# Gated attention and routed experts on one core: three small moves in the order (block 38's scatters, stage 0's block sums, the turning of z)

## The chip, the cores and the metric

One Trainium2 chip, of which the kernel uses one core. The metric is the time of one execution on the device in microseconds (us), and less is better. Every time below is of that core. TensorE (PE) multiplies, VectorE (DVE) and ScalarE (ACT) work elementwise and read TensorE's sums out of PSUM, GpSimd (POOL) and SyncE (SP) mostly start transfers here, and ScalarE starts some as well.

## The reference

Two parts follow each other, all of it in fp32.

```python
# attention: u, v are 8 x 2496 x 256, z is 8 x 2496 x 64
scores = (1 / 2496) * z @ z.T            # per batch
out = maximum(scores, 0) ** 2 @ v
x = (u * out).reshape(19968, 256)
# experts: E = 8, D = 256, F = 1024
expert = token_ids * 2654435761 % 8
for e in range(8):
    mask = expert == e
    y[mask] = maximum(x[mask] @ w1[e], 0) @ w2[e]
```

## The kernel before

The whole program is one order written out by hand: each engine carries out its instructions in the order in which the source issues them, and waits only on data and on buffers that are still in use. A DMA waits also for an earlier one: the transfers that SP and ScalarE start take eight completion semaphores in turn, and each waits until the transfer that held its semaphore before has landed.

**Attention** takes 200 steps: 8 batches, in each of them 5 groups of queries g, in each of them 5 groups of keys s, so 25 steps a batch. A step is worth about 7.2 us. All products are made in the way of Strassen and Winograd: a 2 x 2 block product from 7 products, with block sums before and after. For a step:

- `score` (L251 to L264) makes z z^T on TensorE, relu and square on ScalarE and VectorE. Scores are symmetric, so only the groups with s >= g are made. Where s > g, VectorE transposes them too (`mirror`, L291, 8 transposes), SP stores the result in DRAM (`keep`, L299 and L303), and the later step that has s and g exchanged fetches it on ScalarE's queue (`recall`, L307).
- `sums` (L275 to L278) makes the four block sums t of the scores on VectorE. Scores, sums and mirrors stand two steps ahead of their use (`AHEAD = 2`).
- `attend` (L326) adds the 7 products with v to PSUM. After 5 steps `join` (L339 to L345) puts the products together.
- After that, the rows are turned (`gate`), go through DRAM, are multiplied by u (L389), and GpSimd scatters each row to a slot of its expert (`sort`, L411).

z must stand with its 64 features on the partitions, and twice, on partitions 0 to 63 and 64 to 127. For each batch it comes in four chunks of blocks of 32 rows, all of them during the batch before: `load_z` (L166, two DMAs on SP) loads a chunk, `turn_z` (L186 and L188) transposes it on VectorE, `copy_z` (L193, one DMA on SP) copies it to the other 64 partitions. Chunk c is loaded at step 5 + 4c of the batch before; the turn and the copy follow by a number of steps that the tuple below sets:

```python
for after, do in ((0, load_z), (5, turn_z), (6, copy_z)):
    c, due = divmod((g - 1) * NT + pos - after, 4)
```

**Experts.** The tokens lie in 40 blocks of 512 slots, each of one expert, and one small block of 128. Stage i does the up product of block i (`up_big`, L982: 14 products of two matmuls on TensorE, in two halves of 7) between the down products of block i-1 (7 products). The strings in `ORDER` fix how they alternate; each letter is one product:

```python
ORDER = {"first": "UUUUGUUUGUUUUUUU", "second": "DUDUDUUDUUDUU" "XUxUDUXUDUUUU", ...
         "end": "DDDDDDDd"}
```

"first" is stage 0, in which no down product is there yet; its G finishes the last rows of attention (L398 and L404), whose accumulators were still to be joined. Every set of 7 products ends up in `products`: the first product is copied by ScalarE (L944), and VectorE adds the others (L946 with product 6, L951 with 7, L952 with 5, L959 with 3, L962 with 4). They are made in the order 1, 6, 7, 5, 2, 3, 4. Product 2 is added onto product 1 in its PSUM bank and product 3 onto product 5, so product 3, the sixth, waits until VectorE has read product 5 (L952). After each half ScalarE has done relu, and VectorE makes the block sums of the hidden units (L993 to L996, tile `hs`), which the down products of the next stage read.

A down product has two forms. `down_big` (L1021, 4 matmuls of 256 columns) makes the output transposed; VectorE turns it (L1033, 4 transposes a block), GpSimd writes it to DRAM (L1037, 4 DMAs) and reads it back as rows (L1039), and scatters four tiles of 128 rows to the output (`store`, L934). `down_last` (L1053, 8 matmuls of 128 columns) has the hidden units as weights, so rows come out directly, in tile `o_last`, which has one buffer. It scatters two tiles as soon as its sixth product is joined (L959), two after the seventh (L962). Block 39 alone uses it. The small block's output (tile `o`) comes last: ScalarE's copy (L1090) and one scatter.

Of the kernel before, what the change touches and what calls it, by code (L numbers as in the profile page):

```python
# [24 lines left out]
def kernel(  # L25
# [10 lines left out]
    nc = tc.nc  # L36

    B, S, D = u.shape
# [18 lines left out]
    NL = E * -(-N // (E * BLK))  # L57
# [84 lines left out]
    FQ = FP // 2  # L142
# [582 lines left out]
    def big(j):  # L725
        return j < NL
# [6 lines left out]
    def half(j):  # L733
        return len(slot_tiles(j)) * P // 2
# [66 lines left out]
    def recall_early(i):  # L801
        if i < len(steps) and steps[i][2] < steps[i][1]:
            scores[i] = recall(*steps[i])
# [33 lines left out]
    for i, (b, g, s) in enumerate(steps):  # L837
        pos = i % NT
        to_keep, mirrors = mirrors, []
        if i:  # L840
            a = prepare_scores(i + AHEAD)
            recall_early(i + AHEAD + 1)
        for m in to_keep:
            keep(*m)
        if b + 1 < B:
            for after, do in ((0, load_z), (5, turn_z), (6, copy_z)):
                c, due = divmod((g - 1) * NT + pos - after, 4)
                if not due and 0 <= c < NZ:
                    do(b + 1, c)
        if pos == 0:  # L850
            acc = [acc_ps.tile([P, 2, W], F32, name="acc", tag="acc") for _ in range(4)]
        attend(b, g, s, ready.pop(i), acc, pos == 0, pos == NT - 1)
        if not i:
            a = prepare_scores(i + AHEAD)
            recall_early(i + AHEAD + 1)
        if i == len(steps) - 4:

            x_sb = rowpool.tile([P, 2, 2, D], F32, name="x_row", bufs=3)
            for _ in gate_at_once(*done, x_sb, lambda: mm_ps.tile([P, 2, D], F32, name="g_ps", tag="mm")):
                pass  # L860
            to_sort += [(*done[:2], x_sb, k) for k in range(4)]
        if 0 <= i - (len(steps) - 3) < SURE:
            for _ in turn_x(i - (len(steps) - 3)):
                pass
        if pos == NT - 1:
            done = (b, g, join(g, acc, opool if i < len(steps) - 1 else late, i == len(steps) - NT - 1))
        prepare_mirror(i + AHEAD, a)
        for c in range(max(b, 1), min(b + 2, B)):
            if i - c * PER in LOAD_V:
                load_v(c, LOAD_V[i - c * PER], nc.scalar)  # L870
            if i - c * PER in ADD_V:
                add_v(c, ADD_V[i - c * PER])
        if 0 <= i < NT - 2:
            add_v(0, i + 2)
        if pos == 0 and done is not None and i < len(steps) - NT:
            gated = gate(*done)
        if pos == 1 and gated is not None:
            put(*gated)
            put_at = i
            waiting.append(gated[:2])  # L880
            gated = None

        if i == len(steps) - NT:
            assert not [x for x in waiting + [y[1][:2] for y in fetched] + [y[:2] for y in to_sort] if x < (B - 1, LATE)]
            closing["z and mirrors"].close()
            gpool = pool("gpool", 2, side="right", reuse_waits="tile")
            late = closing["late"].enter_context(tc.tile_pool(name="late", bufs=1, side="right", reuse_waits="tile"))
            for j in range(SURE):
                load_x(j)
        if i in ROUTE and not is_routed:  # L890
            is_routed = next(routed, True) is True
            if is_routed:
                assert i < PREPARE[0] - 1

                rowpool = attention.enter_context(tc.tile_pool(name="rowpool", bufs=2))
        elif is_routed:
            if fetched and i >= fetched[0][0] + (5 if i < len(steps) - NT else 2):
                rows = fetched.pop(0)[1]
                multiply(*rows)
                to_sort += [(*rows, k) for k in range(4)]  # L900
            for _ in range(min(2, len(to_sort))):
                sort(*to_sort.pop(0))
            if len(fetched) < 2 and waiting and (i % PER in FETCH or i >= len(steps) - 5 * NT) and (len(waiting) > 1 or i > put_at + 1):
                fetched.append((i, fetch(*waiting.pop(0))))
        for _ in range((1 + (i % NT == 2)) * is_routed):
            if entered < C:
                enter(entered)
                entered += 1
        for part, after in enumerate((0, 3, 4, 6)):
            if i - after in PREPARE:  # L910
                prepare(PREPARE.index(i - after), part)
        if i == len(steps) - 20:
            load_w(0, 0)
        if i == len(steps) - 2:
            load_w(1, 0)
        if i == len(steps) - NT - 1:
            load_u(b, g)
        if i == len(steps) - 4:
            load_u(b, g, late)
# [43 lines left out]
        done(c21, 1, 0)  # L963
        yield

    def up_big(j):
        x, t = xT[j]
        y11, y12, y21, y22 = (x[:, h, c] for c in range(DP) for h in range(2))
        t1, t2, t3, t4 = (t[:, i] for i in range(4))
        n = half(j)  # L970
        h = hpool.tile([P, 2, 2, FQ, 2 * P], F32, name="h")[:, :, :, :, 0:n]
        sums = hpool.tile([P, 3, FQ, 2 * P], F32, name="hs")[:, :, :, 0:n]
        hid[j] = h, sums
        take = {1: (0, y11), 2: (2, y21), 3: (6, y22), 4: (3, t4), 5: (4, t1), 6: (5, t2), 7: (1, t3)}
        for f in range(0, FQ, 2):
            def made(m, ps):
                first = ps is None
                if first:
                    ps = up_ps.tile([P, 2, 2 * P], F32, name="h_ps", tag="held" if m in (1, 5) else "other")[:, :, 0:n]
                k, y = take[m]  # L980
                for r in range(2):
                    nc.tensor.matmul(ps[:, r], w1[j][:, k, ts(f + r, P)], y, start=first and r == 0,  # L982
                                     stop=True, skip_group_check=True)
                return ps
            r = rpool.tile([P, 2, 2, 2 * P], F32, name="r")[:, :, :, 0:n]
            c = lambda i, k: h[:, i, k, f:f + 2]
            yield from products(
                made, r[:, 0], r[:, 1], c(0, 0), c(0, 1), c(1, 0), c(1, 1),
                lambda o, i, k, ps=None: nc.scalar.activation(o, o if ps is None else ps, AF.Relu))  # L989

            x11, x12, x21, x22 = c(0, 0), c(1, 0), c(0, 1), c(1, 1)
            s1, s2, s4 = (sums[:, i, f:f + 2] for i in range(3))
            nc.vector.tensor_add(s1, x21, x22)  # L993
            nc.vector.tensor_sub(s2, s1, x11)
            nc.vector.tensor_sub(x21, x11, x21)
            nc.vector.tensor_sub(s4, x12, s2)  # L996

    def down_factors(j):
        h, sums = hid[j]
# [85 lines left out]
    def down_small(j):  # L1085
        ps = down_ps.tile([P, D], F32, name="o_ps", tag="any")
        for f in range(FP):
# [7 lines left out]

    ORDER = {"first": "UUUUGUUUGUUUUUUU", "second": "DUDUDUUDUUDUU" "XUxUDUXUDUUUU",
             "other": "UuUDUuUXDUdUDU" "UDUDUxUDUXUDU", "end": "DDDDDDDd"}

# [7 lines left out]
    for i in range(NL + 1):  # L1108
        parts = {}
        for j in at(i):  # L1110
            parts["U" if big(j) else "u"] = (up_big if big(j) else up_small)(j)
        for j in at(i - 1):
            parts["D" if big(j) else "d"] = (down_small if not big(j) else down_last if j == NL - 1 else down_big)(j)
        for j in at(i + 1):
            if i:
                parts["X" if big(j) else "x"] = turn_x(j)
        if i == 0:
            x_sb = late.tile([P, 2, 2, D], F32, name="x_row")
            parts["G"] = gate_at_once(*done, x_sb, lambda: down_ps.tile([P, 2, D], F32, name="g_ps", tag="held", bufs=2))
        for p in ORDER["first" if i == 0 else "second" if i == 1 else "end" if i == NL else "other"]:  # L1120
            next(parts.get(p, iter(())), None)
        for p in parts.values():
            assert next(p, None) is None and next(p, "end") == "end"
        if i == 0:
            for k in range(4):
                sort(*done[:2], x_sb, k)
            closing["late"].close()
            w2pool = pool("w2pool", 2, reuse_waits="tile")
            load_w(0, 1)
        for j in at(i + 2):  # L1130
            load_x(j)
        for m in range(2):
            for j in at(i + 2 - m):
                load_w(j, m)
# [5 lines left out]
    with tc.For_i(0, n_others, 1) as n:  # L1140
# [13 lines left out]
        h = hpool.tile([P, FP, P], F32, name="h1")  # L1154
# [42 lines left out]
```

## Time and profile before

| | before |
|---|---|
| median of 3 runs | 2437.59 us (2437.32 to 2439.12) |
| the profiled execution | 2437.5 us, its span 2435.7 us |
| granted clock of TensorE | 0.998 |
| busy: TensorE, VectorE, ScalarE, GpSimd | 2420.6, 1817.4, 728.5, 717.2 us |
| attention to experts | first expert product starts at 1444.79 us |
| last matmul ends | 2427.0 us |
| last scatter starts | 2430.69 us |

The profile is of one execution. In a line of the timeline the first number is the start and the second the duration (instructions of one kind that follow each other stand in one line), and in brackets stands the idle time of the engine before it and what ended that. A list of waits gives total, times and the longest.

### The profile page before, as it was taken

The numbers are of one execution on the slowest core, as the hardware profiler recorded it, in microseconds if no ns is written. First come the engines' busy times: TensorE is split into PE (matmuls) and PEld (weight loads), VectorE is DVE, ScalarE is ACT, GpSimd is POOL, SyncE is SP. The second block draws the span as 40 slices with busy tenths as digits, with TensorE's granted clock in tenths as the row PEclk, the third lists the DMA queues.
The fourth block names the chain that finished last, engine by engine and source line by source line (L and its number), as shares of the span: only waits on it lengthen the run. The fifth ranks groups of instructions, "written<-read, shape, count | busy, mean of one in ns | idle before, by whom it ended". The sixth has DMA issues, their size and how long they took to land. (4 is left out here: it accounts for less than half of the span.)

```text
span 2435.7 us, 32709 instructions
## 1 busy us (share of the span) xinstructions
PE 2420.6 (99%) x11191; PEld 2013.4 (83%) x11191; DVE 1817.4 (75%) x3811; ACT 728.5 (30%) x1210; POOL 717.2 (29%) x742
## 2 busy tenths in 40 slices
PE   9999999999999999999999999999999999999998
PEld 7787787787787787787787788888888888888887
DVE  7788778869869869768778667777777777777774
ACT  4324314324224224224224212222222222222221
POOL 0002013433534424513411121333232323232324
PEclk9999999999999999999999999999999999999999
DMA  7866667798888788778778677777767686867683
GB/s 151 204 204 188 162 193 234 238 282 243 256 265 253 252 251 255 243 221 245 253 216 258 188 230 232 223 256 221 260 213 264 217 260 215 261 219 256 224 269 116
DMA packets 425193, 559.59 MB, mean 230 GB/s; under 512 B 257372, under 2 KB 350381, under 8 KB 406592
## 3 DMA queue, kind: packets, MB, share of 16 engines
q1 hardware_dynamic: 350704, 326.23, 47.7%
q0 software_dynamic: 41872, 133.39, 15.7%
q10 hardware_dynamic: 32448, 97.86, 12.1%
q8 instruction: 88, 1.44, 0.2%
q14 instruction: 81, 0.66, 0.1%
HBM read 353.28 MB, written 200.26 MB: 227 GB/s over the span
## 5 line engine op out<-in xcount | busy, mean ns | idle before, releaser
L255 ACT ACTIVATE a<-s_ps 128x512 f32<-128x512 f32 (+1 forms) x480 | 246.9, 600 | 696.6 <-PE s_ps L251 614.6
L326 PE MATMUL acc<-t,vc 128*128 128x256 f32 (+3 forms) x1600 | 402.4, 374 | 0.3 <-DVE t L275 0.3
L411 POOL DMA_INDIRECT x_slots<-x_row,row x160 | 203.7, 1273 | 671.0 <-DVE x_row L389 558.7
L326 PEld LDWEIGHTS acc<-a,v_sb 128*128 128x128 f32 (+1 forms) x1600 | 293.2, 190 | 119.4 <-issue 52.7
L326 PE MATMUL acc<-a,v_sb 128*128 128x256 f32 (+3 forms) x1600 | 382.7, 382 | 0.3 <-DVE o L339 0.2
L326 PE MATMUL acc<-t,v_sb 128*128 128x256 f32 (+3 forms) x1600 | 369.7, 373 | 0.0
L326 PEld LDWEIGHTS acc<-t,vc 128*128 128x128 f32 (+1 forms) x1600 | 303.3, 190 | 34.4 <-DVE t L275 0.7
L326 PEld LDWEIGHTS acc<-t,v_sb 128*128 128x128 f32 (+1 forms) x1600 | 303.4, 190 | 33.6
L982 PE MATMUL h_ps<-xs,w 128*128 128x256 f32 x1280 | 316.1, 380 | 0.0
L1021 PE MATMUL o_ps<-h,w 128*128 128x256 f32 x1248 | 294.8, 379 | 0.0
L275 DVE TENSOR_TENSOR t<-a 128x512 f32<-128x512 f32 (+1 forms) x200 | 134.4, 672 | 202.4 <-ACT a L264 139.2
L989 ACT ACTIVATE h<-h 128x512 f32<-128x512 f32 x240 | 151.1, 630 | 420.6 <-DVE h L952 179.1
L982 PEld LDWEIGHTS h_ps<-xs,w 128*128 128x128 f32 x1280 | 243.6, 190 | 32.4
L1021 PEld LDWEIGHTS o_ps<-h,w 128*128 128x128 f32 x1248 | 243.2, 195 | 27.3
L251 PE MATMUL s_ps<-zT 64*128 64x512 f32 (+1 forms) x960 | 238.5, 614 | 0.5 <-DVE zT L186 0.5
L982 PE MATMUL h_ps<-xT,w 128*128 128x256 f32 x960 | 234.9, 380 | 3.3 <-DVE h L952 3.3
L1021 PE MATMUL o_ps<-hs,w 128*128 128x256 f32 x936 | 221.1, 379 | 0.0
L291 DVE STREAM_TRANSPOSE mirror<-a 128x256 f32<-128x256 f32 x640 | 217.8, 409 | 3.5 <-DMA scores<-mirror 2.3
L934 POOL DMA_INDIRECT out_dram<-o_sb,idx x156 | 159.2, 1021 | 186.4 <-DMA o_sb<-o 150.7
L662 POOL DMA_INDIRECT slot_tokens<-token,addr x160 | 170.9, 1068 | 133.5 <-DVE addr L650 85.1
L982 PEld LDWEIGHTS h_ps<-xT,w 128*128 128x128 f32 x960 | 182.5, 190 | 28.6 <-DVE h L952 4.1
L326 PE MATMUL acc<-a,vc 128*128 128x256 f32 (+3 forms) x800 | 201.1, 373 | 0.0
(184 smaller groups left out, 2620.1 us busy)
## 6 DMA issues: line engine op xcount, KB each, us to landing
w<-w_blocks SPq DMA_DIRECT2D x80, 1792.0 KB
scores<-mirror SPq DMA_DIRECT2D x192, 256.0 KB
a<-scores ACTq DMA_DIRECT2D x48, 1024.0 KB
scores<-mirror SPq DMA_DIRECT2D x224, 128.0 KB
a<-scores ACTq DMA_DIRECT2D x32, 896.0 KB
w_blocks<-w POOLq DMA_DIRECT2D x16, 1792.0 KB
xq<-x_slots SPq DMA_DIRECT2D x160, 128.0 KB
o<-y POOLq DMA_DIRECT2D x156, 128.0 KB
```

The source lines that it names most:

```text
L251: nc.tensor.matmul(flat(ps)[:, 0:2 * w].rearrange("p (q c) -> p q c", q=2), tile_of_keys(b, h, s, j), q_h, start=True, stop=True)
L255: nc.scalar.activation(of[:, :, j, h].rearrange("p m q e -> p q m e"), flat(ps)[:, 0:2 * w].rearrange("p (q m e) -> p q m e", q=2, e=in_bl ...
L275: nc.vector.tensor_sub(t1, y12, y11)
L291: nc.vector.transpose(to, in_blocks(a, g)[:, :, j, h].rearrange("p i q (r t) -> p t i q r", t=2)[:, t])
L326: nc.tensor.matmul(acc[k][:, half, 0:w], x[0:n, j, :], y[0:n, j], start=(first and j == 0 and half == 0), stop=(last and j == 1), skip_gro ...
L411: st = nc.gpsimd.indirect_dma_start(out=x_dram[:, :], out_offset=bass.IndirectOffsetOnAxis(ap=row[0:m, c:c + 1], axis=0), in_=x_sb[0:m, q, ...
L662: st = nc.gpsimd.indirect_dma_start(out=slot_dram[:, None], out_offset=bass.IndirectOffsetOnAxis(ap=addr[0:n, to:to + 1], axis=0), in_=tok ...
L934: st = nc.gpsimd.indirect_dma_start(out=out[:], out_offset=bass.IndirectOffsetOnAxis(ap=idx[:, col:col + 1], axis=0), in_=o, in_offset=Non ...
L982: nc.tensor.matmul(ps[:, r], w1[j][:, k, ts(f + r, P)], y, start=first and r == 0, stop=True, skip_group_check=True)
L989: lambda o, i, k, ps=None: nc.scalar.activation(o, o if ps is None else ps, AF.Relu))
L1021: nc.tensor.matmul(ps[:], w2_block(w2[j], k)[:, f], x[:, f], start=first and f == 0, stop=f == FQ - 1, skip_group_check=True)
```

## The change

There are three edits.

1. `down_last` serves the last two blocks, 38 and 39, instead of 39 alone. Block 38's 7 down products become 8 matmuls of 128 columns each, with the operands exchanged; its four transposes and its way through DRAM (5 DMAs on GpSimd) are gone; its four scatters start straight from `o_last`.
2. In stage 0 alone, the block sums of the hidden units are made once over all four columns (4 instructions of 128 x 1024) after the second half, instead of twice over two columns (2 x 4 instructions of 128 x 512), the first of which stood between the halves.
3. z's chunks are turned 3 steps after their load instead of 5, and copied 4 steps after it instead of 6.

Nothing else in the order is touched, apart from the completion semaphores, which are dealt out anew as transfers move or vanish.

```diff
-            for after, do in ((0, load_z), (5, turn_z), (6, copy_z)):
+            for after, do in ((0, load_z), (3, turn_z), (4, copy_z)):
...
-    def up_big(j):
+    def up_big(j, sums_last=False):
...
+        def add(a, b):
+
+            x11, x12, x21, x22 = (h[:, k, i, a:b] for i in range(2) for k in range(2))
+            s1, s2, s4 = (sums[:, i, a:b] for i in range(3))
+            nc.vector.tensor_add(s1, x21, x22)
+            nc.vector.tensor_sub(s2, s1, x11)
+            nc.vector.tensor_sub(x21, x11, x21)
+            nc.vector.tensor_sub(s4, x12, s2)
+
         for f in range(0, FQ, 2):
...
-            x11, x12, x21, x22 = c(0, 0), c(1, 0), c(0, 1), c(1, 1)
-            s1, s2, s4 = (sums[:, i, f:f + 2] for i in range(3))
-            nc.vector.tensor_add(s1, x21, x22)
-            nc.vector.tensor_sub(s2, s1, x11)
-            nc.vector.tensor_sub(x21, x11, x21)
-            nc.vector.tensor_sub(s4, x12, s2)
+            if not sums_last:
+                add(f, f + 2)
+        if sums_last:
+            add(0, FQ)
...
-            parts["U" if big(j) else "u"] = (up_big if big(j) else up_small)(j)
+            parts["U" if big(j) else "u"] = up_big(j, i == 0) if big(j) else up_small(j)
...
-            parts["D" if big(j) else "d"] = (down_small if not big(j) else down_last if j == NL - 1 else down_big)(j)
+            parts["D" if big(j) else "d"] = (down_small if not big(j) else down_last if j >= NL - 2 else down_big)(j)
```

## The prediction

> **What bounds the kernel now.** I read the page first, then TensorE's waits, then the timelines of three places: the seam between attention and experts, the tail, and the moments at which VectorE turns z.
>
> ```profile
> PE 2420.6 (99%) x11191; PEld 2013.4 (83%) x11191; DVE 1817.4 (75%) x3811; ACT 728.5 (30%) x1210; POOL 717.2 (29%) x742
> ```
>
> TensorE is busy for 2420.6 of 2435.7 us; 15.1 us are idle. The list of TensorE's waits says where (total, times, longest):
>
> ```profile
> PE h_ps L982 <- DVE h L952: 3.3, 2, 2.5
> ...
> PE o_ps L1053 <- DVE ro L946: 0.6, 1, 0.6
> ...
> PE acc L326 <- DVE t L275: 0.3, 1, 0.3
> PE acc L326 <- DVE o L339: 0.2, 1, 0.2
> ```
>
> The waits come to 6.3 us, and most of the rest, 8.7 us, is the tail after TensorE's last matmul (2435.7 - 2427.0). In attention it does not stand still: 0.5 us over 200 steps. So only the seam's 2.5 us and the tail can be won, and attention can only be lost. The profiled execution took 2437.5 us around its span of 2435.7, 0.1 from the median (2437.59); I sum against 2437.5. A measurement of this kernel can tell about 0.2% from no change, 4.9 us: faster means under 2432.7, slower over 2442.5.
>
> **Part one, stage 0's block sums.** TensorE's timeline at the seam (start, duration, last the idle time before):
>
> ```profile
> 1456.22 1.03 PE L982 MATMUL h_ps<-xT,w 128*128 128x256 f32 x4
> 1459.74 1.99 PE L982 MATMUL h_ps<-xT,w 128*128 128x256 f32 x4 [2.50 <-DVE h L952]
> 1461.52 1.90 PE L982 MATMUL h_ps<-xs,w 128*128 128x256 f32 x4
> 1463.23 1.92 PE L1021 MATMUL o_ps<-h,w 128*128 128x256 f32 x8
> ```
>
> VectorE meanwhile, and below it, from the table by stretch, the time after the gap (busy times of the engines; then granted clock, DMA share, GB/s):
>
> ```profile
> 1454.90 0.68 DVE L993 TENSOR_TENSOR hs<-h 128x512 f32<-128x512 f32 x1
> ...
> 1456.82 0.69 DVE L996 TENSOR_TENSOR hs<-h,hs 128x512 f32<-128x512 f32 x1
> 1457.42 0.68 DVE L946 TENSOR_TENSOR r<-r,h_ps 128x512 f32<-128x512 f32 x1
> ...
> 1459.00 0.69 DVE L952 TENSOR_TENSOR h<-h,h_ps 128x512 f32<-128x512 f32 x1
> 1459.80:1463.30 3.50, 3.50 (x9) 2.79 (x10) 0.69 (x1) 1.67 (x3) 0.00 (x0) 0.51 0.50 117
> ```
>
> Four sums (L993 to L996) stand for 2.52 us ahead of the three additions that release the bank TensorE needs. The edit moves them behind: L946 then begins at 1454.90, L952 ends at 1457.17, and the product that started at 1459.74 starts near 1457.22. It is due at 1457.09, so a wait of 0.14 stays, with the 0.10 that a start after a wait takes longer (1.13 instead of 1.03 after the 0.79 gap at 1450.94).
>
> The clock is the second term. After the gap the table shows 0.51 granted, over 3.5 us. Two products cost 1.78 and 1.71 us (from start to start, 1459.74 to 1461.52 to 1463.23) instead of 0.865: 1.76 more. After the 0.79 gap the next product followed 0.96 later, at full pace. The Trainium skill ("TensorE: Matmul & The Clock Gate", Part 1, HAM oscillation) warns of idle gaps over about 3.4 us only; by that rule the 2.50 gap would not be what halves the clock, the halving could stay, and the gain below would be 1.8 us smaller. The row halves it after 2.50, at once; I go by the row.
>
> What the edit adds comes later: four sums over 128x1024. The nearest row is L260's 128x1024 multiplication, 1.22 us each. With L962 over by about 1459.9, the first runs 1459.9 to 1461.1 and the second, which needs it, to 1462.3. It feeds block 0's second down product, now due at 1461.64 (1457.22 + 0.97 + 0.865 + 1.73 + 0.865): a new wait of 0.74 us plus 0.10, too short for the clock by the 0.79 row. It starts at 1462.4, where it started at 1465.85: **3.4 us gained**. The third sum (1463.5) comes before the third down product (1465.1). Bounds: 1.6 if the half clock stays, 4.0 if the sums overlap better. Weights in time: w2 of block 0 landed at about 1453.6.
>
> **Part two, block 38's way out.** The tail on GpSimd:
>
> ```profile
> 2410.45 2.68 POOL L1037 DMA_DIRECT2D o<-y  x4 [8.21 <-DVE y L1033]
> 2416.00 0.78 POOL L1039 DMA_DIRECT2D o_sb<-o  x1 [2.87 <-issue]
> 2420.38 1.04 POOL L934 DMA_INDIRECT out_dram<-o_sb,idx  x1 [3.60 <-DMA o_sb<-o]
> ...
> 2429.41 0.97 POOL L934 DMA_INDIRECT out_dram<-o_last,idx  x1 [0.30 <-issue]
> 2430.69 0.97 POOL L934 DMA_INDIRECT out_dram<-o,idx  x1 [0.30 <-issue]
> ```
>
> Nine scatters follow each other at 1.28 us from 2420.38: the queue is the limit, because block 38 goes through DRAM. Without the detour (5 transfers, 4 VectorE transposes) block 38's four scatters go at about 2406.6, 2407.9, 2410.0 and 2411.3, behind L959 and L962. Block 39's first two go at 2422.7 and 2423.9, after L959 (2422.25), the others at 2425.2 and 2426.5. GpSimd is free at 2427.5, and the last store waits for ScalarE's copy instead (2427.62 + 0.37): 2428.3 to 2428.4. The end follows the last store by 5.0 us (2435.7 - 2430.69). That is 2.3 to 2.4 us.
>
> Against it: block 38's 7 products become 8 matmuls of 128 columns. Down_last's products show 1.78 to 1.82 us, down_big's 1.73, so 0.05 to 0.09 each, 0.4 to 0.6 together. For it: VectorE's two transposes at 2409.38 (0.77 us) no longer delay L994, which keeps TensorE 0.3 us at 2412.1. TensorE ends 0.05 to 0.25 later. Net **2.25 us gained** (1.5 to 2.5). Both blocks share one o_last buffer: block 39's first write (L951, 2416.42) must wait for block 38's last scatter to have read, at 2411.3 + about 2.1, so 2413.5: 3 us of cover. Were it gone, L951 would hold TensorE's bank.
>
> **Part three, z turned and copied two steps sooner.** Nothing waits for z in time to be released, so the gain is none. The cost: the turn has 3 steps (7.2 us each) after its load instead of 5, and VectorE stands until the load lands. It already does at 5 steps (first VectorE's waits, then lines of the timelines of VectorE, ScalarE's queue and SP):
>
> ```profile
> DVE zT L186 <- DMA zn<-in_z_dram: 25.9, 7, 6.6
> 696.50 0.76 DVE L186 STREAM_TRANSPOSE zT<-zn 64x256 f32<-64x256 f32 x2 [7.54 <-issue]
> 683.62 0.38 ACTq L307 DMA_DIRECT2D a<-scores  x1
> 691.63 1.10 SPq L166 DMA_DIRECT2D zn<-in_z_dram  x2
> ```
>
> The third of four chunks (step 13 of a batch's 25) is the tight one; the others land 8 us or more ahead of their need. Behind the turn stand 8 mirror transposes and the next sum: 0.47 wake, 0.98 turn, 2.64 mirrors, 0.73 sum, together 4.82 us. TensorE needs that sum at 155.8, 335.1, 514.5, 693.8, 873.5, 1052.8, 1232.1 (batches 1 to 7), so z must be there 4.8 earlier. By the single packets it landed at 151.7, 330.4, 515.8, 696.0, 872.2, 1050.9, 1231.6. With these landings TensorE would stand 0.8, 0.1, 6.1, 7.0, 3.6, 2.9 and 4.3 us.
>
> But they will not be these. SP issues the load behind mirror stores, and a DMA waits for the transfer eight back that held its semaphore. In batches 3 to 5 that was the recall of step 21 (issued 683.62, z only at 691.63). With the copies moved, the order of semaphores shifts by one in the built program: the load now waits for the recall of step 20 at most, which landed at 146.2, 323.3, 503.6, 682.9, 862.4, 1042.0, 1221.6. Add 0.4 to issue, and 4.8 to 5.9 us of flight beside the next recall (batch 1: 146.94 to 151.72; batch 2: 324.50 to 330.40). Against the need that leaves 0 to 0.4 us of stall in each of the batches 1 to 5. Batches 6 and 7 flew 7.1 and 8.2 us behind three mirror stores that now go sooner; they come within need at up to 5.6 and 5.3 us. **0 to 1.5 us lost, taken as 0.3**, since most of the flights end within need. A load that met no recall flew 2.7 us (batch 5, 869.58 to 872.24), one beside it 5.9 (batch 2). The Trainium skill ("DMA: Bandwidth & Descriptors", Issuing engines are not separate DMA queues) says the same of all issuers: their transfers interleave on the same 16 engines; by it every load would fly 5.9 and the whole 1.5 us be lost.
>
> **The rivals.** *Slower: z lands too late.* If the loads land as before, the stalls add to 25 us, and five are over 2.5 us, so the clock adds five times 1.76: 33 us, about 2465; with some batches spared, 2445 to 2458. It decides once z lands over 6.0 us after the recall of step 20 in most batches. For it: VectorE waits 25.9 us today. Against it: that wait stems from a semaphore order that changes.
>
> *No change: the seam's wait only moves.* If the clock halves anyway, or the wide sums bring a wait that halves it again, part one gives 1.6: 2437.5 - 1.6 - 2.25 + 0.3 = 2434.0.
>
> *No change: the tail stays.* If o_last's reuse holds block 39, the last stores queue as before and part two gives nothing: 2434.4. The same band holds one or two late z loads (2436 to 2442).
>
> **How the numbers follow.** Forecast: 2437.5 - 3.4 - 2.25 + 0.3 = 2432.2 us, chance 0.55. Its own range is 2430.7 to 2435.9: all the better ends give 2437.5 - 4.0 - 2.5 = 2431.0, less 0.3 for the lowest run of before under its median; all the worse ones 2437.5 - 1.6 - 1.5 + 1.5. Of the 0.55, 0.47 lies under 2432.7. Seam or tail failing: 0.13; a few late z loads: 0.10; z late in most batches: 0.22. So faster 0.47, same 0.31, slower 0.22. The range goes from 2430.7 up to 2445, into the mildest of the slower cases, which leaves some 0.19 out.
>
> **What would show it.** Right: no wait over 1 us at the seam and no stretch at half clock there; GpSimd's last store on ScalarE's copy, without a queue before it; no `acc <- t` waits in attention. Wrong: TensorE waiting for t (L275) some 7 times, 150 to 1232 us in, each behind a late turn; or o_last's first addition ending an idle time of TensorE.

## The result: 1.4% slower, all of it in attention

| | before | after |
|---|---|---|
| median | 2437.45 us (2437.20 to 2439.12, 4 runs) | 2472.94 us (2472.07 to 2474.74, 4 runs) |
| the profiled execution, its span | 2437.5, 2435.7 us | 2472.07, 2470.2 us |

The ratio after to before is 1.0143, 95% interval 1.0129 to 1.0156. The forecast was 2432.2 us, its range 2430.7 to 2445, and the rival "z lands too late" was priced at about 2465. One execution of an experiment's kernel (e10) took 3776 us at a granted clock of 0.63; it is not in the ratio given for that kernel.

The page of the changed kernel: TensorE's busy time, which counts a product at half clock as a longer one, grew by 10.0 us, the span by 34.5.

```profile
PE 2430.6 (98%) x11247; PEld 2021.0 (82%) x11247; DVE 1815.3 (73%) x3803; ACT 727.7 (29%) x1210; POOL 696.1 (28%) x737
```

TensorE's list of waits (total, times, longest) has the line that the prediction named as its refutation. Before, the first two lines read 0.3 and 0.2, once each, and the third did not exist:

```profile
PE acc L326 <- DVE t L275: 16.0, 7, 3.4
PE acc L326 <- DVE o L339: 7.6, 6, 4.6
PE acc L326 <- DVE addr L650: 3.8, 1, 3.8
...
PE o_ps L1028 <- DVE hs L981: 0.6, 1, 0.6
```

VectorE's list names what it stood for; before it was 25.9 us in 7 waits (and 7.5 us in one put down to "issue"). Two of the waits, 4.7 us together, stand at the program's start in both kernels:

```profile
DVE zT L186 <- DMA zn<-in_z_dram: 107.7, 14, 13.3
```

One such place, batch 4, in the timelines of VectorE and TensorE, and in the table by stretch around it (granted clock third from the end):

```profile
711.49 0.77 DVE L186 STREAM_TRANSPOSE zT<-zn 64x256 f32<-64x256 f32 x2 [13.25 <-DMA zn<-in_z_dram]
712.19 0.36 DVE L188 STREAM_TRANSPOSE zT<-zn 64x224 f32<-64x224 f32 x1
712.48 2.68 DVE L291 STREAM_TRANSPOSE mirror<-a 128x256 f32<-128x256 f32 x8
715.09 0.64 DVE L275 TENSOR_TENSOR t<-a 128x512 f32<-128x512 f32 x1
...
715.79 2.08 PE L326 MATMUL acc<-t,vc 128*128 128x256 f32 x4 [3.39 <-DVE t L275]
717.66 1.53 PE L326 MATMUL acc<-a,vc 128*128 128x256 f32 x4
719.02 1.03 PE L326 MATMUL acc<-t,vc 128*128 128x256 f32 x4
...
715.20:718.60 3.40, 2.81 (x7) 2.28 (x8) 3.37 (x8) 0.00 (x0) 0.32 (x1) 0.51 0.87 191
```

VectorE stands 13.25 us for the chunk, then does the turn, the eight mirror transposes and the first sum, and TensorE waits for that sum. What follows the wait runs at half clock for 3.4 us.

The seam and the tail went as said. TensorE at the seam, then GpSimd's last scatters:

```profile
1493.56 2.12 PE L992 MATMUL h_ps<-xT,w 128*128 128x256 f32 x8
1495.52 1.03 PE L992 MATMUL h_ps<-xs,w 128*128 128x256 f32 x4
1496.38 1.89 PE L1028 MATMUL o_ps<-h,w 128*128 128x256 f32 x8
1498.11 1.03 PE L992 MATMUL h_ps<-xT,w 128*128 128x256 f32 x4
1499.72 1.99 PE L1028 MATMUL o_ps<-hs,w 128*128 128x256 f32 x8 [0.59 <-DVE hs L981]
```

```profile
2445.43 1.03 POOL L934 DMA_INDIRECT out_dram<-o_last,idx  x1 [0.30 <-issue]
2457.30 0.97 POOL L934 DMA_INDIRECT out_dram<-o_last,idx  x1 [10.84 <-issue]
...
2462.41 0.97 POOL L934 DMA_INDIRECT out_dram<-o,idx  x1 [0.30 <-ACTq L1148]
```

The 2.50 us gap is gone, 0.59 us came; and GpSimd's last four tiles start when block 39 is ready, no longer behind block 38's. The span split at landmarks of the timelines gives the account:

| stretch | before | after | difference |
|---|---|---|---|
| start to the end of attention's last product with v | 1444.95 | 1483.02 | +38.07 |
| to block 0's second down product | 20.90 | 16.70 | -4.20 |
| to the end of TensorE's last matmul | 961.18 | 961.59 | +0.41 |
| to the start of the last scatter | 3.66 | 1.10 | -2.56 |
| to the end of the span | 5.01 | 7.77 | +2.76 |
| sum | 2435.70 | 2470.18 | +34.48 |

Of the 38.07, TensorE's waits in attention make 27.0 (27.2 against 0.2, without the 0.3 for t at the program's start that both kernels have). The records of the granted clock hold six stretches of half clock in attention, 23.9 us together, each beginning in such a wait or up to 1.1 us after it; half of that time, less the idle part of it, is the other 11. The forecast took the last row as unchanged.

### The profile page after: what moved, and what is told of

It is laid out like the page before. It is cut to its first block, busy times and chain, and to the rows that moved or that the text cites. A ratio compares the mean times of both kernels' runs of the same rounds, so it can differ in the third digit from the quotient of the medians.

```text
span 2470.2 us, 32786 instructions
## 1 busy us (share of the span) xinstructions
PE 2430.6 (98%) x11247; PEld 2021.0 (82%) x11247; DVE 1815.3 (73%) x3803; ACT 727.7 (29%) x1210; POOL 696.1 (28%) x737
## 4 chain that ended last, share of the span: by engine, by line
PE 90%; DMA 4%; DVE 3%; issue 1%; SPq 1%; ACT 0%; POOL 0%; ACTq 0%; DVEq 0%; POOLq 0%
PE acc L326 42%; PE h_ps L992 19%; PE o_ps L1028 19%; PE s_ps L251 9%; DMA a<-scores 2%; DMA zn<-in_z_dram 1%; DVE mirror L291 1%; PE o_ps L1060 1%; DMA x_row<-x 0%; DVE t L275 0%; DVE t L277 0%; DVE t L276 0%; DMA x<-x_sb 0%; DMA zT<-zT 0%; DMA v_sb<-in_v_dram 0%
## 5 line engine op out<-in xcount | busy, mean ns | idle before, releaser
L326 PE MATMUL acc<-t,vc 128*128 128x256 f32 (+3 forms) x1600 | 408.7, 378 | 19.8 <-DVE t L275 16.0
L411 POOL DMA_INDIRECT x_slots<-x_row,row x160 | 185.3, 1158 | 707.5 <-DVE x_row L389 592.0
L1028 PE MATMUL o_ps<-h,w 128*128 128x256 f32 x1216 | 287.3, 379 | 0.0
L1028 PEld LDWEIGHTS o_ps<-h,w 128*128 128x128 f32 x1216 | 236.8, 195 | 26.5
L1028 PE MATMUL o_ps<-hs,w 128*128 128x256 f32 x912 | 215.5, 379 | 0.6 <-DVE hs L981 0.6
```

The lines of the kernel that those rows point to most:

```text
L326: nc.tensor.matmul(acc[k][:, half, 0:w], x[0:n, j, :], y[0:n, j], start=(first and j == 0 and half == 0), stop=(last and j == 1), skip_gro ...
L411: st = nc.gpsimd.indirect_dma_start(out=x_dram[:, :], out_offset=bass.IndirectOffsetOnAxis(ap=row[0:m, c:c + 1], axis=0), in_=x_sb[0:m, q, ...
L1028: nc.tensor.matmul(ps[:], w2_block(w2[j], k)[:, f], x[:, f], start=first and f == 0, stop=f == FQ - 1, skip_group_check=True)
```

## The experiments

Each was run beside the kernel before on the same chip; the medians of before in the five groups were 2438.6, 2438.5, 2439.8, 2441.0 and 2439.0 us, with single runs from 2435.9 to 2452, so a difference of 1 us is not told by a median here, and I go by the ratio's interval and by the profile.

**The three edits apart.** First z alone (e1), on the kernel before:

```diff
-            for after, do in ((0, load_z), (5, turn_z), (6, copy_z)):
+            for after, do in ((0, load_z), (3, turn_z), (4, copy_z)):
```

> The kernel before with z turned 3 and copied 4 steps after its load, nothing else. Theory A (all of the loss is z): the expert part starts 38.1 us later, as in the changed kernel, so 2437.5 + 38 = 2475 us (2472 to 2478), with six stalls of TensorE of 2.3 to 3.8 us for t and half clock behind each. Rival B (the loss needs the new tail or the new sums as well, through the completion semaphores dealt out anew): under 2460 us.

Measured 2472.6 us, ratio 1.0132 (1.0117 to 1.0148); attention ends at 1482.93 us, 38.0 later than before. Theory A holds: z is the whole loss. (How it is shared among the waits differs from one execution to the next: 0.5 to 4.8 us each.)

Then the expert edits with z as before (e2; in the changed kernel the tuple goes back to 5 and 6), the seam alone (e3; also `down_last if j >= NL - 1`), and the tail alone (e4; e2 with `up_big(j)`, so without sums last):

> The changed kernel with z turned and copied at 5 and 6 steps, as before. Theory A: attention as before, the seam 4.2 us shorter, block 38 0.4 longer, the last store 2.6 sooner behind TensorE: 2437.5 - 6.4 = 2431.1 us; if the end of the program again waits 2.9 us longer for a fetch of instructions (theory F), 2434.0. Rival B (part of the loss is in the expert part): over 2437.5.

> Only stage 0's block sums moved behind its products. Theory: the wait of 2.50 us and the two products at half clock are gone, a wait of 0.6 comes: 2437.5 - 4.2 = 2433.3 us, the end of the program as before. Rival (the forecast's sum was right and the surplus of 0.8 in the changed kernel was chance): 2434.1. Rival (the wide sums cost later stages): 2436 or more.

> Only block 38 through the row form. Theory: TensorE ends 0.4 us later, the last store starts 2.2 sooner. If the long drain at the end (3.7 instead of 0.9 us) belongs to GpSimd's shorter program, 2437.5 - 2.2 + 2.9 = 2438.2 us; if it came from other edits or by chance, 2435.3.

Measured: seam and tail together (e2) 2436.8 us, ratio 0.9988 (0.9979 to 0.9997); the seam alone 2436.8, 0.9989 (0.9980 to 0.9998); the tail alone 2438.0, 0.9994 (0.9985 to 1.0003). That is a gain of about 0.1% in the first two, so rival B falls; the intervals hold the expected gains of 3.5 us (e2 with the long end) and 4.2 us (e3), but the medians say 1.8 in both. In the third no difference can be told. The profiles add what the times hide. In all three, attention ended 1.8 to 3.4 us later than in the profile of before, although nothing in it was changed (the waits of TensorE there, for the join near 700 us and for z's copy near 733 and 914 us, 0.3 to 0.8 us each, make 0.9 to 1.4 us of it; the rest is not accounted for); before's own runs on that chip spread over 8 us. The last row of the account is 7.75 us in both kernels with the new tail and 5.03 in the one without. And the seam of the tail-only kernel, which has the old sums and the old gap, looks like this:

```profile
1460.50 1.13 PE L992 MATMUL h_ps<-xT,w 128*128 128x256 f32 x4 [2.50 <-DVE h L952]
1461.46 1.03 PE L992 MATMUL h_ps<-xs,w 128*128 128x256 f32 x4
1462.33 1.89 PE L1028 MATMUL o_ps<-h,w 128*128 128x256 f32 x8
```

The same 2.50 us gap, and full clock behind it: the stretch to the second down product takes 18.16 us, not 20.90. So of the gain of 4.20 only 1.5 is surely the edit's. The half clock made 1.8, in executions in which it comes; the other 0.9 is a wait of 0.79 us of the profile of before, at 1450.94, which e4 and the changed kernel lack and the seam-only kernel has (0.95).

**What makes z late.** Four kernels, all with the expert edits. Only the copy goes back (e5), `(3, turn_z), (6, copy_z)`:

> The changed kernel with z still turned at 3 steps, but copied at 6 as before. Theory A (VectorE's turn stands ahead of the block sums and waits for a load that has not landed): no better than the changed kernel, 2470 to 2476 us, six or seven waits of TensorE for t. Rival C (SP stands at the early copy and holds mirror stores and with them recalls): the loss is gone, about 2434 us.

Measured 2475.1 us, 1.0129 (1.0101 to 1.0156), VectorE's wait for z 107.2 us, TensorE's for t 17.3. Rival C falls: it is the turn in VectorE's queue, not the copy in SP's.

One step more lead (e6), `(4, turn_z), (5, copy_z)`:

> The changed kernel with z turned at 4 and copied at 5 steps, one step (about 7 us) more than in the change. Theory A: in the changed kernel TensorE stood 2.3 to 3.8 us a batch, and 7 us more cover that, so TensorE does not wait for t, and the time is that of the change without z: 2434 to 2437 us. Rival D (it is not the load's landing but the new order of semaphores, which is about the same here): 2455 us or more.

Measured 2441.2 us, 0.9998 (0.9984 to 1.0013): nearly all of the 35 us are back; the ratio lies 0.0010, some 2 us, above that of the expert edits alone. VectorE waits 57.7 us for z, and TensorE stands 2.0 to 2.7 us in three batches, so the expected absence of stalls was wrong by a little; rival D falls. One step is worth almost the whole loss, which is what a threshold looks like.

The load two steps sooner as well (e7), `(-2, load_z), (3, turn_z), (4, copy_z)`:

> The changed kernel with the loads two steps sooner as well, so that the turn is 5 steps behind the load as before, at the place of the change. Theory A: the third chunk is then loaded at step 11, ahead of the three recalls of steps 19 to 21; no stall, 2434 to 2437 us. Rival E (the place of the turn and the copy itself costs, whatever the lead): 2455 us or more.

Measured 2434.9 us, 0.9980 (0.9967 to 0.9993). VectorE's list:

```profile
DVE zT L186 <- DMA zn<-in_z_dram: 4.6, 2, 3.8
```

These two are at the program's start; in the steps VectorE does not wait for z at all. The place of the turn costs nothing, so rival E falls. The third chunk alone back at 5 and 6, the others at 3 and 4 (e8):

```diff
-            for after, do in ((0, load_z), (3, turn_z), (4, copy_z)):
+            for after, do in ((0, load_z), (3, turn_z), (4, copy_z), (5, turn_z), (6, copy_z)):
...
-                if not due and 0 <= c < NZ:
+                if not due and 0 <= c < NZ and (not after or (c == 2) == (after > 4)):
```

> The changed kernel with only the third chunk of z turned and copied at 5 and 6 steps again, the other three at 3 and 4. Theory A with the forecast's claim that the third chunk alone is tight: 2434 to 2437 us. Rival (the other chunks are late as well, as VectorE's waits of 6 us for the fourth chunk in batches 6 and 7 suggest): 2440 to 2455 us.

Measured 2439.0 us, 0.9992 (0.9979 to 1.0005). The claim holds for the loss: without the third chunk it is gone to within what can be told. It does not hold to the letter: VectorE waits 60.8 us in 16 pieces now, the fourth chunk among them (4 to 10 us each), and one wait of TensorE of 2.4 us for a sum is left.

The load sooner, the turn where it was before, `(-2, load_z), (5, turn_z), (6, copy_z)` (e10); and the early load and turn alone on the kernel before, without the expert edits (e12):

> All the edits to the experts, z loaded two steps sooner and turned and copied where it was before, so that the turn is 7 steps behind the load. Theory A: nothing waits for z; 2434.9 us as with the early turn (2433.5 to 2436.5). Rival (the early turn itself gains, for it takes VectorE's 34 us of waits out of the way): 1 us or more slower than that.

> The kernel before with z loaded, turned and copied two steps sooner, nothing else. Theory A: with its lead kept, the earlier turn costs nothing, and since VectorE no longer stands for z (33 us before), the small waits of TensorE in attention of some executions go too: 2438.5 - 0 to 2 us. Rival E (an early turn costs by its place): over 2445.

Measured 2437.0 us, 0.9984 (0.9971 to 0.9996), and 2437.5, 0.9990 (0.9980 to 1.0000). Between e10 and e7's 0.9980 no difference can be told, and e12 is not slower than before: the earlier turn, once its data is there, neither gains nor costs anything measurable. Only the lead counts.

Then the question why three steps, 21 us, are not enough for a load whose flight takes 3 to 11 us. The load stays at its step and moves to ScalarE's queue (e14, the changed kernel otherwise):

```diff
-                    do(b + 1, c)
+                    do(b + 1, c, *([(nc.scalar,)] if do is load_z else []))
```

> The changed kernel, z's loads of the later batches started on ScalarE's queue instead of SP's, at the same step of the order, turned and copied at 3 and 4. Theory H (3 steps are enough; the load is late because SP's queue stands some 30 us behind the order, at mirror stores that wait for the recall of step 20): the third chunk is issued some 30 us sooner against TensorE's step, VectorE does not wait for it, no wait of TensorE for t, 2434 to 2438 us. Rival (the flight itself beside recalls and stores is too long for 3 steps): the stalls stay, over 2455 us.

Measured 2433.0 us, 0.9969 (0.9956 to 0.9982), with the change's own turn at 3 steps: better than both kernels of the case. The third chunk of batch 2, SP's issue and VectorE's turn in the changed kernel, then ScalarE's issue in this one:

```profile
331.32 0.88 SPq L166 DMA_DIRECT2D zn<-in_z_dram  x2
339.15 0.77 DVE L186 STREAM_TRANSPOSE zT<-zn 64x256 f32<-64x256 f32 x2 [10.35 <-DMA zn<-in_z_dram]
```

```profile
288.11 0.96 ACTq L166 DMA_DIRECT2D zn<-in_z_dram  x2
```

Written at the same step, started 43 us sooner (35 us sooner against TensorE's step 13, since the changed kernel was 8 us behind by then); it landed at 293.1 and was turned at 320.6 without a wait. Over the seven batches ScalarE starts this chunk 36 to 46 us ahead of the times of SP in the profile of before. Theory H holds: the lead in steps was there, but SP's queue is late (it starts the load of step 13 32 to 40 us after TensorE began that step in the profile of before, 29 to 35 us in that of the changed kernel), as it stands at stores and loads whose semaphores the recalls hold. SP's list of waits in the changed kernel has these three among its lines:

```profile
SPq L303 <- DMA a<-scores: 205.0, 23, 13.1
SPq L299 <- DMA a<-scores: 146.4, 15, 14.4
SPq L166 <- DMA a<-scores: 40.8, 6, 14.9
```

The first two are the mirror stores, the third is z's load itself. The semaphores are dealt out anew in e14 as well, so it does not tell apart what the other queue brought and what the other semaphores brought. The flights are not short (5.0 to 11.0 us in this kernel), only no one waits for them.

**Where the tail's 2.56 us went.** GpSimd's sequencer ends the program with a drain. From its records, after the last scatter's start:

| kernel | drain begins | lasts | span ends |
|---|---|---|---|
| before, e1, e3, e11, e12 | 3.3 | 0.89 | 5.0 |
| after, e2, e4 to e10, e14 (all with the new tail) | 3.2 | 3.75 | 7.75 |

The early z and the seam without the new tail (e11: e7 with `down_last if j >= NL - 1`), for what the tail is worth:

> The kernel with early loads, without the new tail: z loaded, turned and copied two steps sooner, and the seam's sums last. If the new tail is worth nothing, since the drain takes 2.7 us of the 2.6 that the scatters gain and TensorE ends 0.3 later, it takes as long as with the tail: 2434.5 to 2435 us; if the tail is worth the forecast 2.25 us, 2437.

Measured 2434.8 us, 0.9978 (0.9968 to 0.9989), against 0.9980 with the tail: the new tail is worth nothing that can be told. Four kernels ask why. Two clearings ahead of the last scatter, `nc.gpsimd.memset(fill[:], 0.0)`, on e7 (e9):

> The kernel with early loads and all the edits (e7), with two clearings of a 128x1024 tile on GpSimd (0.94 us each in the profile of before) put ahead of the very last scatter. In every profile with the new tail the program ends 7.75 us after the last scatter's start, in every one without it 5.0. Theory G (the end hangs on GpSimd's sequencer, which runs ahead of a busy engine but stands at ScalarE's copy when the queue is empty): the last scatter starts 1.9 us later, the drain is again short, and the end comes 5.0 after the start: 2.7 - 1.9, that is 0 to 1 us sooner than without the clearings, at about 2434. Theory F (the shorter program ends in a fetch or the like): the drain stays at 3.7 us and the end comes 1.9 us later, 2436.8.

Measured 2436.3 us, 0.9990 (0.9981 to 0.9999); the drain stays at 3.75 us, the end at 7.75. The sequencer did not run ahead of the clearings (it read its next operand 0.5 us before the scatter's start, as with an empty queue), so this spoke for F without excluding G. The old tail with copies ahead of ScalarE's last one, eight (e13) and then sixteen (e15):

```diff
+        for _ in range(16):
+            nc.scalar.copy(fill[:].rearrange("p (f n) -> p f n", f=4), hid[j][:, 0:4])
         nc.scalar.copy(o[:], ps[:])
```

> The kernel before (old tail, GpSimd's program unchanged) with eight copies of 128x512 on ScalarE (0.6 us each by L989's row) ahead of the small block's last copy, so that GpSimd's scatter queue runs empty and its sequencer stands at ScalarE's copy. ScalarE's eight copies can begin only after the hidden units of the small block, so the last copy comes 0 to 5 us later. Theory G (the long drain comes when the last scatter is let go late by ScalarE, whatever the program): the end lies 7.75 us after the last scatter's start. Theory F (it belongs to the shorter GpSimd program of the new tail): 5.0 us after it.

> As the kernel with eight copies on ScalarE ahead of the last one (e13), with sixteen: there the last copy ended at 2431.4, still before GpSimd's turn for the last scatter at 2432.66. Eight more, 0.6 us each, put it near 2436, with GpSimd's queue empty since 2432.4. Theory G (a late release makes the long drain): the end 7.75 us after the last scatter's start, near 2444. Theory F (the program with the new tail has it, whatever the release): 5.0 to 5.2 us, near 2441.5.

With eight the last scatter still kept its turn (one execution, 2439.7 us), which decides nothing. With sixteen (one execution, 2438.5 us; the copies began early, so the last one ended at 2431.37, not at 2436) the scatter did wait for ScalarE with the queue empty:

```profile
2430.05 0.98 POOL L934 DMA_INDIRECT out_dram<-o_last,idx  x1 [0.30 <-issue]
2431.64 0.97 POOL L934 DMA_INDIRECT out_dram<-o,idx  x1 [0.62 <-ACTq L1143]
```

The drain took 0.89 us and the end came 5.02 us after the start. A late release does not make the long drain, so G falls. Last, e14 with five transfers put back on GpSimd (e16):

```diff
+        if j == NL - 2:
+            spare = nc.dram_tensor("spare", (5, P, P), F32)
+            for k in range(5):
+                nc.gpsimd.dma_start(out=spare[k], in_=ident[:])
```

> The kernel with z's loads on ScalarE's queue (e14), and in place of block 38's five transfers that the new tail removed, five of 64 KB from a constant tile to a spare tensor, on GpSimd behind block 38's scatters (they add nothing to the output). Theory F (the long drain comes with the shorter program): the drain is 0.9 us again and the time 2.9 us less, 2430.1. Theory G: the drain stays at 3.7 us and the time at 2433.

Measured 2432.5 us, 0.9971 (0.9959 to 0.9984): GpSimd has its 725 transfers of before again, and the drain takes 4.15 us. That it hangs on their number falls too, and with it theory F in the form of a shorter program. A fetch of instructions does not part the two cases by itself: the records of DMA packets hold one 2.3 to 2.4 us after the last scatter's start in all eleven profiles with the long drain, but also one at 2.05 us (e15) and one at 3.74 us (e1) with the short drain. The long drain is in every profile with the new tail (eleven of eleven) and in none of the seven without; what in it does that stays open.

## Why the prediction was wrong, point by point

- **What bounds the kernel: right.** Attention could only be lost, and it was.
- **Part one: right in kind, the clock term not as argued.** The wait for the second sum came as forecast (0.59 us, 0.74 expected); L946 to L952 run as placed, and even the 0.14 us wait ahead of product 3 came: products 2 and 3 at 1493.56 take 2.12 us together instead of 1.89, that is 0.13 of wait and 0.10 for the start after it (waits under 0.15 us are not listed). The gain was 4.20 us for 3.4, but 0.9 of it is luck, a wait that the profile of before happened to have. But I wrote that the row halves the clock "after 2.50, at once": of the six profiles with the old seam and its 2.50 us gap, it is halved behind it in four (before, e1, e12, e15) and not in two (e4, e13). That term should have stood as a chance; what decides it is in the last section. The bound of 1.6 was meant for a clock that stays halved; 1.5 is what the edit gains where it was not halved before.
- **Part two: right up to the last scatter.** The last scatter starts 1.10 us behind TensorE, 2.56 sooner; 0.41 was paid on TensorE for 0.05 to 0.25 expected. The step that failed is "the end follows the last store by 5.0 us": I took a number of the old program as a constant, and it became 7.77. Nothing is left of 2.25: by the rows of the account (+0.41, -2.56, +2.76) the tail lost 0.6.
- **Part three: wrong, and with it the sign.** The step that failed is "0 to 0.4 us of stall in each of the batches 1 to 5", through two of its terms. "Add 0.4 to issue": against the recall of step 20's own issue the load was issued 2.9 to 7.8 us later; the forecast's times make 4.4 to 6.1, and in batches 3 to 5 it was 6.7 to 7.8. "4.8 to 5.9 us of flight": measured 4.7, 7.0, 5.7, 7.2, 6.9, 8.1 and 10.7. The sooner start put the load beside the recall of step 21: the two were issued within 1.8 us of each other in batches 1 to 6, where in the profile of before the load came 6 to 8 us behind it in batches 3 to 5. Two smaller ones: VectorE began 0.8 to 2.0 us after the landing (0.47 taken), and in batches 1 and 2 routing work (L547 and L645 to L650, 2.8 and 3.2 us) stood behind the turn too, which the chain of 4.82 us did not have. Had step 20's recall flown as long as in the profile of before, z would have landed 5.2 us behind it in batch 1 and 7.4 to 8.6 us in the others; the forecast's own dividing line was 6.0.
- **The rival was the case.** "z lands too late" had the place, the mechanism and nearly the price: 25 us of stall and 9 of clock forecast, 27.0 and 11 measured. Its chance of 0.22 was the error. The trace showed VectorE already standing for this load with 5 steps of lead; a margin that is used up today, in 6 of 7 batches (all but batch 2), is not saved by a sum of the best flights seen. With the flights that batches 6 and 7 showed (7.1 and 8.2 us) in all batches, the sum would have given stalls everywhere.
- **The Trainium skill's two places.** "DMA: Bandwidth & Descriptors", Issuing engines are not separate DMA queues, spoke against the short flights, and the runs agree with it: the loads beside recalls flew up to 10.7 us, and in e14, from another queue, up to 11.0. "TensorE: Matmul & The Clock Gate", Part 1, describes a free-running window of about 3.4 us, and the traces agree: the stretches of half clock behind the waits are 3.41 or 6.83 us long, and their starts lie on one grid (last section). Its rule of idle gaps over about 3.4 us is too mild here: in the changed kernel every wait of 2.9 us and more was followed by half clock, though the wait was shorter than the window in three of six cases.

## What to carry to other kernels

A lead counted in steps of the program is a lead in time only if the queue that issues the load is on time: compare the step at which a load is written with the time at which its engine starts it, and if an in-order queue is 35 us late behind stores, move the load to another queue or further ahead before moving its consumer nearer. Where a consumer already waits for its data, the next step of lead that is taken away comes off the critical engine, and each wait of 2 to 3 us there may cost 1.7 us more in clock (half of a stretch of 3.41). And a gain at the very end of a program is only a gain if what follows the last transfer stays the same, so the end of the span belongs in the sum as a term with bounds.

## What the runs showed of the hardware that was not expected

Whether a wait of 1.9 to 2.5 us halves the clock depends on where it falls. With z alone the clock was halved behind a wait of 2.03 us (1053 us) and not behind one of 2.19 (1085 us); the changed kernel halved it behind 2.93 and not behind 2.26. The records of the clock show why. In the eight profiles with a stretch of half clock before TensorE's last matmul, all stretches of one execution, the one at the program's end included, start whole multiples of 3.413 us apart (with z alone 52, 57, 54, 97, 63, 67 and 284 of them), whatever the waits are. Cut into pieces on that grid, the 18 profiles have 64 pieces at full clock in which TensorE idles over 0.6 us: half clock follows all 26 with 1.92 us or more, and none of the 38 with 1.89 or less. The seam's 2.50 us lies in one piece in the profile of before (2.50, halved) and is split in e4 (1.78 and 0.72) and e13 (1.55 and 0.95), which kept the full clock; the 2.19 us with z alone are split into 1.89 and 0.30. So the part of a wait in one piece counts, and the place of the grid differs from one execution to the next.

GpSimd's closing drain took 0.89 us in the seven profiles without the new tail, 3.75 us in ten with it and 4.15 us in e16. Neither the late release (e15) nor the number of transfers (e16) decides which; the cause stays open.
